# Who adds up the weights: a fused attention and two-layer feed-forward kernel without accumulating transfers in its input projections

## The chip, the cores and the metric

The kernel runs on one core of a Trainium2 chip. TensorE (PE) multiplies matrices into PSUM banks; VectorE (DVE), ScalarE (ACT) and GpSimd (POOL) work element by element; transfers are issued from SyncE's queue (SP) or from GpSimd's (POOL). The metric is the device time of one execution in microseconds, the median of several runs. Before the change it is 526.03 us (three runs, 525.88 to 526.29).

## The reference

Causal attention over 2 batches, 12 heads, 448 positions and 64 dimensions, and then two feed-forward layers on 896 tokens of 768 features, with 2048 features inside:

```python
attn = softmax(mask(q @ k.T / 8)) @ v
x = attn.transpose(0, 2, 1, 3).reshape(896, 768)
h = x @ w1_in;  x = (h * clip(h + 3, 0, 6) / 6) @ w1_out
h = x @ w2_in;  y = (max(h, 0) + alpha * min(h, 0)) @ w2_out
```

All inputs and the output are float32. The weights reach the kernel as 64-bit words, from which it makes 32-bit ones itself.

## The kernel before

**The arithmetic.** Every float32 operand is split into a high part (fp32r) and a low part, the rest; a product of two operands is three matrix multiplications: high by high, high by low, low by high (`three`, L575 to L590). On top of that each of the four large products is done by a scheme of Strassen's kind: 2 × 2 blocks are multiplied with seven products in place of eight, which needs sums and differences of blocks beforehand. The blocks of the activations are made in `take_x`, those of the weights in `w_in` (L592 to L690) and `w_out` (L692 to L787).

**The input projections.** A layer's `w_in` runs for 8 pairs of weight blocks, `w1` and `w2`, each of 128 × 768. `convert` (L249) loads each one with a transfer from SP's queue into a `raw` buffer, of which there are three, and makes 32-bit words of it with two ScalarE instructions (L262, L265) and one on VectorE (L268). Then there are four sums of 384 columns in a pair. The first two are always on VectorE: `s12[right] = w2[left] + w2[right]` (L599) and `s12[left] = s12[right] + w1[left]` (L601). The other two, `w1[right] += s12[left]` and `w2[left] += w1[left]` (L626 and L627), go through the helper `add_on` (L301): either GpSimd issues a transfer inside SBUF that adds on arrival (L307), or VectorE adds (L309). In the trace the first of the two as a transfer is `wf<-s`, the second `wf<-wf`. What comes out is split into high and low parts: ScalarE rounds (L617), VectorE subtracts (L618). Seven products per pair fill three PSUM banks, `a`, `b` and `c`, by turns; ScalarE's copies (L319, L321) and VectorE's additions (L650) empty them, and L660 to L670 apply the activation. The results are the tiles `g`.

**The output projections.** `w_out` makes sums of 768 columns of the weights (`onto`, L702) and of 448 columns of `g` (`add_g`, L728) through the same `add_on`, and differences on VectorE (L707); it splits them (L283, L290) and adds up seven products over 16 tiles. L770 adds finished banks to `y`.

**The order.** Nothing is written in the order in which it runs. Each step is an `Op` with a list of engines and an estimate for each; `Plan.solve` (L113) simulates the engines with these estimates and fixes the order and the engine of each instruction. A step's due time is worked out backwards from the steps that need it, less the estimate of the first engine in its list, and for a transfer less its landing estimate (L119 to L122). For `add_on` the landing estimate is `WAIT[cols]` plus 0.0025 us per column; for a load it is the two numbers in `.lands(2.3, 1.9)`. Where a step may go either way, it is a transfer if that would be done 3.0 us (`EARLY`) before its due time, and otherwise goes to the engine that would be done first:

```python
if POOL in o.dma and done_by(*o.on[0]) + o.on[-1][1] <= o.due - EARLY:
    ok = e == POOL
else:
    ok = e == min(o.on, key=lambda c: done_by(*c))[0]
```

`SEEDS` is a list of random seeds: the first one draws two settings of the planner and shifts the due times of all the attention's steps, each of the others shifts those of some of them. The engines then run their instructions strictly in the order that the plan gave each, and semaphores make them wait for one another.

The functions as they were before the change, with the line numbers of the profile:

Of the kernel before, what the change touches and what calls it, by code (L numbers as in the profile page):

```python
# [24 lines left out]
W3 = HK * P  # L25
# [7 lines left out]
PE, DVE, ACT, POOL, SP = "PE", "DVE", "ACT", "POOL", "SP"  # L33


def f32(t):
    return t.bitcast(F32)
# [23 lines left out]

ISSUE, WAIT = 0.9, {384: 2.2, 448: 4.6, 768: 4.2}

TURN = {("r", "r"): 0.05, ("r", "t"): 0.17, ("r", "c"): 0.2, ("r", "q"): 0.15, ("r", "m"): 0.15, ("t", "r"): 0.12,
        ("t", "c"): 0.12, ("t", "q"): 0.1, ("m", "c"): 0.2, ("m", "r"): 0.1, ("m", "q"): 0.1}
# [14 lines left out]
class Plan:  # L82
# [4 lines left out]
    def op(self, on, emit, reads=(), writes=(), due=FAR, chain=None, also=(), port=False, mode=None):  # L87

        o = Op(on if isinstance(on, list) else [on], emit, due)
        o.port, o.mode = port, mode  # L90
        for key in reads:
            w, r = self.state.setdefault(key, ([], []))
            o.before.update(w)
            r.append(o)
        for key in writes:
            w, r = self.state.setdefault(key, ([], []))
            o.before.update(w)
            o.before.update(r)
            self.state[key] = ([o], [])
        o.before.discard(o)  # L100
        for key in (*reads, *writes, *also):
            b = key[0] if isinstance(key, tuple) else key
            if b not in o.bufs:
                o.bufs.append(b)
                b.left += 1
        if chain:
            if chain in self.last:
                o.before.add(self.last[chain])
            self.last[chain] = o
        self.ops.append(o)  # L110
        return o
# [127 lines left out]
class Kernel:  # L239
# [9 lines left out]
    def convert(self, src, sign=1.0, halves=False):  # L249

        nc, op = self.nc, self.plan.op
        raw = Buf("raw", "raw", 2 * DM, U32)
        w = Buf("w", "wf", DM, U32)
        keys = [(w, 0), (w, W3)] if halves else [w]

        def words(k):
            return raw.tile.rearrange("p (n two) -> p n two", two=2)[:, :, k]

        op((SP, 0.45), lambda e: nc.sync.dma_start(out=raw.tile, in_=src), writes=[(raw, "l"), (raw, "h")]).lands(2.3, 1.9)


        op((ACT, 0.80), lambda e: nc.scalar.activation(  # L262
            f32(w.tile), f32(words(1)), AF.Prelu, scale=sign * 2.0 ** -112, alpha=-2.0 ** 32), reads=[(raw, "h")], writes=keys)

        op((ACT, LOWEST), lambda e: nc.scalar.activation(  # L265
            words(0), raw.tile.bitcast(U16).rearrange("p (n four) -> p n four", four=4)[:, :, 1],
            AF.Copy, bias=-0.49999, scale=1.0 / 8192.0), writes=[(raw, "l")])
        op((DVE, 0.87), lambda e: nc.vector.scalar_tensor_tensor(  # L268
            out=w.tile, in0=w.tile, scalar=3, in1=words(0), op0=ALU.logical_shift_left, op1=ALU.bitwise_or),
           reads=[(raw, "l")], writes=keys, port=True)  # L270
        return w
# [26 lines left out]
        op(low_on, low, reads=[*keys, hi], writes=[lo], port=not ps)  # L298
        return hi, lo

    def add_on(self, out, cols, dst, src, reads, writes, send=False):  # L301

        nc = self.nc

        def emit(e):
            if e == POOL:
                nc.gpsimd.dma_start(out=dst(), in_=src(), accum_op=ALU.add)  # L307
            else:
                nc.vector.tensor_add(dst(), dst(), src())  # L309

        on = [(POOL, ISSUE), (DVE, 0.065 + 0.00105 * cols)]
        self.plan.op(on[:1] if send else on, emit, reads=reads, writes=writes, port=True).lands(WAIT[cols], 0.0025 * cols, on=POOL)

    def copy(self, out, src, key, cols, sign=1.0):
        nc = self.nc
# [276 lines left out]
    def w_in(self, layer, m, src, due):  # L592
        nc, op = self.nc, self.plan.op
        w1 = self.convert(src[m], -1.0, True)
        w2 = self.convert(src[m + PAIRS], 1.0, True)
        s12 = Buf("w", "s12", DM, F32)
        left, right = slice(0, W3), slice(W3, DM)

        op((DVE, 0.47), lambda _: nc.vector.tensor_add(s12.tile[:, right], f32(w2.tile[:, left]), f32(w2.tile[:, right])),  # L599
           reads=[(w2, 0), (w2, W3)], writes=[(s12, W3)], port=True)  # L600
        op((DVE, 0.47), lambda _: nc.vector.tensor_add(s12.tile[:, left], s12.tile[:, right], f32(w1.tile[:, left])),  # L601
           reads=[(s12, W3), (w1, 0)], writes=[(s12, 0)], port=True)

        def both(name, cols, src, keys):

            if cols == DM:
                hi, lo = Buf("w", name + "h", DM, F32R), Buf("w", name + "l", DM, F32R)
                parts = (hi, 0), (lo, 0)
            else:
                t = Buf("w", name, DM, F32R)  # L610
                parts = ((t, 0), 0), ((t, W3), W3)

            def out(i):
                key, first = parts[i]
                return (key[0] if isinstance(key, tuple) else key).tile[:, first:first + cols]

            op((ACT, 0.07 + 0.00087 * cols), lambda _: nc.scalar.copy(out(0), src()), reads=keys, writes=[parts[0][0]])  # L617
            op((DVE, 0.065 + 0.00105 * cols), lambda _: nc.vector.tensor_sub(out(1), src(), f32(out(0))),  # L618
               reads=[*keys, parts[0][0]], writes=[parts[1][0]], port=True)
            return parts  # L620
# [2 lines left out]
        p56 = both("s12", DM, lambda: s12.tile, [(s12, 0), (s12, W3)])  # L623
        p4 = both("a2", W3, lambda: f32(w2.tile[:, right]), [(w2, W3)])

        self.add_on(w1, W3, lambda: f32(w1.tile[:, right]), lambda: s12.tile[:, left], [(s12, 0)], [(w1, W3)], SEND > 1)  # L626
        self.add_on(w2, W3, lambda: f32(w2.tile[:, left]), lambda: f32(w1.tile[:, left]), [(w1, 0)], [(w2, 0)], SEND > 0)  # L627
        p7 = both("s4", W3, lambda: f32(w1.tile[:, right]), [(w1, W3)])
        p3 = both("s3", W3, lambda: f32(w2.tile[:, left]), [(w2, 0)])

# [167 lines left out]
    def build(self):  # L798
        nc, op, d = self.nc, self.plan.op, self.dram
        start, step = 9.0, 5.8  # L800
        warm = Buf("ps", "warm")
        for _ in range(WARM):
            op((PE, 0.9), lambda _: nc.tensor.matmul(
                warm.tile[:, 0:3 * P], lhsT=self.mask[:, 3 * P:4 * P], rhs=self.mask[:, 3 * P:6 * P], start=True, stop=True),
               writes=[warm], due=-90.0)
        for c in range(KIN):
            self.attend(c, [start + (n + 1) * step for n in (2 * c, 2 * c + 1)])
        self.vary = len(self.plan.ops)
        alpha = Buf("alpha", "alpha")
        op((SP, 0.45), lambda _: nc.sync.dma_start(out=self.alpha, in_=d["alpha"]), writes=[alpha], due=start + 20.0).lands(2.1, 0.1)  # L810
        for sign in (1.0, -1.0):
            at = slice(0, KFF) if sign > 0 else slice(KFF, 2 * KFF)
            op((DVE, 0.2), lambda _, sign=sign, at=at: nc.vector.tensor_scalar(
                self.alpha[:, at], self.alpha[:, at], -sign, sign, ALU.mult, ALU.add), writes=[alpha], due=start + 60.0)
        due = start + 2 * KIN * step - 2.0
        for layer, (w_in, w_out) in enumerate((("w1i", "w1o"), ("w2i", "w2o"))):
            for m in range(PAIRS):
                self.w_in(layer, m, d[w_in], due)
            self.w_out(layer, d[w_out], due, self.turned if layer == 0 else self.store)
# [3 lines left out]
OVER = 38  # L823
WARM = 3
SPLIT = (0, 1)
SEND = 0
LOWEST = 0.85
SCALERS = 2
SEEDS = (21, 46993, 49846, 39502, 10980, 46964, 66667)
ATT = {"kq": 2 * S, "v": 8 * D, "e": 3 * P, "el": 4 * P, "small": 21, "a": 16 * P}  # L830


def solve(k):
    return k.plan.solve(SLOTS, ("u", "w", "raw"), ("u", OVER, set(ATT)), k.vary, SEEDS)

# [105 lines left out]
```

## Time and profile before

| | |
|---|---|
| median of three runs | 526.03 us (525.88 to 526.29) |
| the profiled execution, its own time | 521.06 us |
| its span | 519.0 us |
| mean granted clock of TensorE | 0.99 |
| busy: TensorE, VectorE, ScalarE, GpSimd | 96%, 82%, 75%, 25% |
| chain that ended last | TensorE 44%, VectorE 27%, transfers 17%, ScalarE 5% |
| issues of GpSimd's queue at L307 | 48 of `g`, 38 of `wf` |
| transfers | 82.69 MB, 159 GB/s in the mean |

The span runs from the first to the last instruction of the program; the execution's own time has the start and the end around it, some 2 us. A busy share is the part of the span in which an engine had an instruction in it. A matrix multiplication's end is modelled, so the distance from one start to the next tells more than its length. On VectorE too an instruction begins shortly before the one ahead of it has ended. The attention takes the first 85 us or so; the first layer's input projections follow until about 190, its output projections until about 300, the second layer's until about 405 and the end.

### The profile page before, as it was taken

To read this page: it belongs to the slowest core of one execution; us is meant where nothing else is said; L and a number is where in the kernel's file an instruction comes from. 1 tells how busy PE (TensorE), PEld (TensorE's weight loads), DVE (VectorE), ACT (ScalarE), POOL (GpSimd) and SP (SyncE) were. 2 spreads that over 40 slices of the span, in tenths; PEclk is the share of its full clock that TensorE was granted. 3 is DMA by queue.
4 is the path that set the end of the run, shared out by engine and by line. 5 is a ranking of instruction groups with operands and counts; after the bars stand their busy time and mean duration, and the time that the engine had idled before them with its cause. 6 is when DMAs were issued, how large, how long until landed. Compare 5 with 4: busy or idle time off the path is not lost.

```text
span 519.0 us, 7641 instructions
## 1 busy us (share of the span) xinstructions
PE 496.6 (96%) x2598; PEld 429.2 (83%) x2598; DVE 425.1 (82%) x808; ACT 390.5 (75%) x756; POOL 128.7 (25%) x196
## 2 busy tenths in 40 slices
PE   8899999999799999998998897999999999989997
PEld 4575667989689999997997786889999999979996
DVE  5799989999588799878999986887787999699710
ACT  6999999888588799866966676777788997597101
POOL 2775884112111003621001011221210146200000
PEclk9999999999889999999999899999999999999999
DMA  8655300678766549998005436676764699930111
GB/s 273 261 197 167 90 21 24 189 216 218 188 168 167 192 136 276 256 267 251 11 0 153 136 85 162 188 204 148 198 160 153 200 258 273 249 75 1 54 53 53
DMA packets 27638, 82.69 MB, mean 159 GB/s; under 512 B 3152, under 2 KB 15184, under 8 KB 27600
## 3 DMA queue, kind: packets, MB, share of 16 engines
q1 hardware_dynamic: 15216, 61.76, 34.3%
q0 software_dynamic: 12384, 20.45, 22.4%
q8 instruction: 20, 0.33, 0.3%
q14 instruction: 18, 0.15, 0.1%
HBM read 59.00 MB, written 2.75 MB: 119 GB/s over the span
## 4 chain that ended last, share of the span: by engine, by line
PE 44%; DVE 27%; DMA 17%; issue 5%; ACT 5%; POOL 2%; DVEq 0%; POOLq 0%; ACTq 0%; SPq 0%
PE a L584 12%; PE ya L584 12%; DMA g<-g 8%; PE c L584 7%; DMA wf<-s 6%; DVE wf L268 4%; PE b L584 3%; PE yc L584 3%; PE o L565 2%; PE t L521 2%; PE s L496 2%; DVE e L447 2%; DVE g L662 2%; DMA raw<-w2o 1%; DMA raw<-w1o 1%
## 5 line engine op out<-in xcount | busy, mean ns | idle before, releaser
L307 POOL DMA_DIRECT2D g<-g x48 | 41.6, 925 | 146.2 <-DVE g L668 50.3
L268 DVE SCALAR_TENSOR_TENSOR wf<-wf,raw 128x768 uint32<-128x768 uint32 x64 | 60.9, 952 | 15.1 <-ACT wf L262 14.9
L265 ACT ACTIVATE raw<-raw 128x768 uint32<-128x768 uint16 x64 | 58.5, 916 | 4.5 <-DMA raw<-w2i 1.9
L262 ACT ACTIVATE wf<-raw 128x768 f32<-128x768 f32 x64 | 57.5, 903 | 2.8 <-DVE w3l L287 1.4
L307 POOL DMA_DIRECT2D wf<-wf x25 | 21.8, 871 | 133.5 <-DVE s L599 39.4
L452 ACT ACTIVATE e<-e,small 128x128 f32<-128x128 f32 (+2 forms) x72 | 36.0, 505 | 5.1 <-DVE small L447 4.9
L476 POOL TENSOR_SCALAR e<-e,small 128x256 f32<-128x256 f32 (+2 forms) x67 | 31.4, 492 | 15.6 <-DVE small L469 11.0
L447 DVE CUSTOM_DVE_ANT_0 e<-s,mask 128x384 f32<-128x384 f32 (+2 forms) x72 | 27.0, 419 | 6.1 <-PE s L496 5.5
L618 DVE TENSOR_TENSOR s<-wf,s 128x384 fp32r<-128x384 f32 x32 | 17.8, 570 | 10.2 <-ACT s L617 10.2
L319 ACT COPY o<-ya 128x448 f32<-128x448 f32 x3 | 1.6, 533 | 31.6 <-PE ya L584 31.6
L617 ACT CAST s<-wf 128x384 fp32r<-128x384 f32 x32 | 16.1, 507 | 12.0 <-DMA wf<-s 10.2
L565 PE MATMUL o<-a,v 128*64 128x448 f32 (+3 forms) x192 | 23.4, 386 | 0.0
L617 ACT CAST s12h<-s 128x768 fp32r<-128x768 f32 x16 | 13.3, 834 | 13.1 <-DVE s L601 13.1
L565 PEld LDWEIGHTS o<-a,v 128*64 128x64 f32 x192 | 12.7, 136 | 12.6 <-issue 5.2
L496 PE MATMUL s<-kq 64*128 64x384 f32 (+2 forms) x144 | 21.7, 405 | 1.3 <-DMA kq<-kq 0.8
L618 DVE TENSOR_TENSOR s12l<-s,s12h 128x768 fp32r<-128x768 f32 x16 | 15.8, 988 | 7.2 <-ACT s12h L617 6.7
L521 PE MATMUL t<-ident,e 128*128 128x128 f32 x144 | 19.0, 278 | 1.6 <-DVE small L447 1.1
L521 PEld LDWEIGHTS t<-ident,e 128*128 128x128 f32 x144 | 15.5, 141 | 5.5 <-POOL e L476 2.4
L496 PEld LDWEIGHTS s<-kq 64*128 64x128 f32 x144 | 11.6, 186 | 9.2 <-DVE small L447 3.2
L307 POOL DMA_DIRECT2D wf<-s x13 | 11.2, 864 | 25.3 <-DVE s L618 10.7
L668 DVE SCALAR_TENSOR_TENSOR g<-r,alpha,g 128x448 f32<-128x448 f32 x24 | 16.3, 679 | 0.9 <-ACT r L666 0.8
L319 ACT COPY g<-a 128x448 f32<-128x448 f32 x16 | 8.5, 531 | 10.3 <-PE a L584 10.1
(830 smaller groups left out, 1771.3 us busy)
## 6 DMA issues: line engine op xcount, KB each, us to landing
raw<-w1i SPq DMA_DIRECT2D x16, 768.0 KB, 5.4
raw<-w1o SPq DMA_DIRECT2D x16, 768.0 KB, 4.4
raw<-w2i SPq DMA_DIRECT2D x16, 768.0 KB, 4.5
raw<-w2o SPq DMA_DIRECT2D x16, 768.0 KB, 5.0
g<-g POOLq DMA_DIRECT2D x48, 224.0 KB, 9.1
kq<-kq SPq DMA_DIRECT2D x11, 448.0 KB, 5.3
wf<-wf POOLq DMA_DIRECT2D x10, 384.0 KB, 8.8
v<-v SPq DMA_DIRECT2D x12, 256.0 KB, 2.7
```

Source lines behind the costliest of these rows:

```text
L262: op((ACT, 0.80), lambda e: nc.scalar.activation(f32(w.tile), f32(words(1)), AF.Prelu, scale=sign * 2.0 ** -112, alpha=-2.0 ** 32), reads= ...
L265: op((ACT, LOWEST), lambda e: nc.scalar.activation(words(0), raw.tile.bitcast(U16).rearrange("p (n four) -> p n four", four=4)[:, :, 1], A ...
L268: op((DVE, 0.87), lambda e: nc.vector.scalar_tensor_tensor(out=w.tile, in0=w.tile, scalar=3, in1=words(0), op0=ALU.logical_shift_left, op1 ...
L307: nc.gpsimd.dma_start(out=dst(), in_=src(), accum_op=ALU.add)
L447: nc.vector.tensor_tensor_reduce(out=view(), in0=t.tile[:, off:off + cols], in1=self.mask[:, at:at + cols], scale=-SCALE, scalar=3.0e38, o ...
L452: nc.scalar.activation(view(), view(), AF.Exp, bias=small.tile[:, u:u + 1], scale=-1.0, accum_out=small.tile[:, 7 + u:8 + u])
L476: (nc.gpsimd if e == POOL else nc.vector).tensor_scalar(view(), view(), by, 1.0, ALU.mult, ALU.mult)
L496: nc.tensor.matmul(t.tile[:, off:off + (i + 1) * P], lhsT=kq.tile[rows, S + i * P:S + (i + 1) * P], rhs=kq.tile[rows, 0:(i + 1) * P], star ...
L521: nc.tensor.transpose(t.tile[:, at * P:(at + 1) * P], src.tile[:, off:off + P], self.ident)
L565: nc.tensor.matmul(o.tile[side * D:(side + 1) * D, 0:cols], lhsT=v.tile[:, (2 * kc + side) * D:(2 * kc + side + 1) * D], rhs=a.tile[:, at: ...
L584: nc.tensor.matmul(out, lhsT=t.tile[:, first + at:first + at + P], rhs=rhs.tile, start=start and key is hi and rhs is xh, stop=stop and ke ...
L618: op((DVE, 0.065 + 0.00105 * cols), lambda _: nc.vector.tensor_sub(out(1), src(), f32(out(0))), reads=[*keys, parts[0][0]], writes=[parts[ ...
```

## The change

Four things change. `add_on` gets a third setting: `send` below 0 leaves VectorE alone in the list of engines. `w_in` uses it (`SEND = -1`), so all four sums of a pair are VectorE's. The planner's estimates for transfers become longer: `WAIT` from 4.6 to 6.5 us for 448 columns, from 4.2 to 7.0 for 768 (that for 384 has no use any more), and a load's from 2.3 + 1.9 to 3.2 + 2.4; one ScalarE step of `convert` is counted 0.81 in place of 0.85 us. And the seeds are others, four in place of seven, the first one kept.

```diff
-ISSUE, WAIT = 0.9, {384: 2.2, 448: 4.6, 768: 4.2}
+ISSUE, WAIT = 0.9, {384: 6.0, 448: 6.5, 768: 7.0}
...
-        op((SP, 0.45), lambda e: nc.sync.dma_start(out=raw.tile, in_=src), writes=[(raw, "l"), (raw, "h")]).lands(2.3, 1.9)
+        op((SP, 0.45), lambda e: nc.sync.dma_start(out=raw.tile, in_=src), writes=[(raw, "l"), (raw, "h")]).lands(3.2, 2.4)
...
-        op((ACT, LOWEST), lambda e: nc.scalar.activation(
+        op((ACT, 0.81), lambda e: nc.scalar.activation(
...
-    def add_on(self, out, cols, dst, src, reads, writes, send=False):
+    def add_on(self, out, cols, dst, src, reads, writes, send=0):
...
-        self.plan.op(on[:1] if send else on, emit, reads=reads, writes=writes, port=True).lands(WAIT[cols], 0.0025 * cols, on=POOL)
+        self.plan.op(on[:1] if send > 0 else on[1:] if send < 0 else on, emit, reads=reads, writes=writes, port=True).lands(WAIT[cols], 0.0025 * cols, on=POOL)
...
-        self.add_on(w1, W3, lambda: f32(w1.tile[:, right]), lambda: s12.tile[:, left], [(s12, 0)], [(w1, W3)], SEND > 1)
-        self.add_on(w2, W3, lambda: f32(w2.tile[:, left]), lambda: f32(w1.tile[:, left]), [(w1, 0)], [(w2, 0)], SEND > 0)
+        self.add_on(w1, W3, lambda: f32(w1.tile[:, right]), lambda: s12.tile[:, left], [(s12, 0)], [(w1, W3)], SEND)
+        self.add_on(w2, W3, lambda: f32(w2.tile[:, left]), lambda: f32(w1.tile[:, left]), [(w1, 0)], [(w2, 0)], SEND)
...
-SEND = 0
-LOWEST = 0.85
+SEND = -1
-SEEDS = (21, 46993, 49846, 39502, 10980, 46964, 66667)
+SEEDS = (21, 41862, 63962, 88307)
```

## Rows read from the trace of the kernel before

**Rows 1.** The page, part 1: busy time, share of span, instructions of each engine.

```profile
PE 496.6 (96%) x2598; PEld 429.2 (83%) x2598; DVE 425.1 (82%) x808; ACT 390.5 (75%) x756; POOL 128.7 (25%) x196
```

**Rows 2.** Stretches: length, busy us per engine (instructions), granted clock, DMA share, GB/s.

```profile
0.00:85.00 85.00, 80.46 (x596) 50.72 (x597) 69.97 (x260) 76.90 (x235) 55.86 (x112) 1.00 0.46 154
85.00:130.00 45.00, 44.70 (x219) 40.70 (x218) 44.27 (x73) 39.26 (x66) 7.03 (x9) 1.00 0.65 187
130.00:190.00 60.00, 56.26 (x257) 50.41 (x257) 46.02 (x73) 47.79 (x80) 7.74 (x9) 0.94 0.61 170
190.00:240.00 50.00, 49.95 (x242) 45.07 (x241) 42.75 (x65) 38.28 (x63) 18.27 (x21) 1.00 1.01 263
240.00:300.00 60.00, 55.00 (x263) 50.21 (x262) 58.50 (x92) 44.58 (x74) 4.30 (x5) 0.97 0.31 86
300.00:345.00 45.00, 41.56 (x201) 37.10 (x200) 35.18 (x57) 32.10 (x55) 6.93 (x8) 1.00 0.60 164
345.00:400.00 55.00, 55.00 (x273) 50.98 (x272) 43.42 (x68) 42.73 (x72) 9.49 (x11) 1.00 0.62 171
```

**Rows 3.** Waits: who waited for whom, us in total, times, longest.

```profile
ACT s L617 <- DMA wf<-s: 10.2, 4, 3.9
DVE s L618 <- ACT s L617: 10.2, 4, 4.2
...
PE a L584 <- ACT g L321: 5.5, 4, 3.1
PE ya L584 <- DVE y L770: 3.7, 1, 3.7
PE ya L584 <- DVE w6l L290: 2.9, 3, 1.3
PE a L584 <- DVE g L650: 1.8, 1, 1.8
```

**Rows 4.** The chain in order of time: start, us, what; the transfers `wf<-s`.

```profile
125.22 6.30 DMA wf<-s
135.24 6.47 DMA wf<-s
...
312.26 8.21 DMA wf<-s
```

**Rows 5.** Timeline: start, us, instruction, in brackets the idle time before it.

```profile
131.54 0.51 ACT L617 CAST s<-wf 128x384 fp32r<-128x384 f32 x1 [2.52 <-DMA wf<-s]
...
141.74 0.51 ACT L617 CAST s<-wf 128x384 fp32r<-128x384 f32 x1 [3.41 <-DMA wf<-s]
...
143.48 0.48 PE L584 MATMUL a<-t200h,s12h 128*128 128x448 f32 x1 [1.94 <-ACT g L321]
...
320.55 0.51 ACT L617 CAST s<-wf 128x384 fp32r<-128x384 f32 x1 [3.87 <-DMA wf<-s]
```

**Rows 6.** DMA issues of GpSimd's queue: count, KB each, median us to landing.

```profile
g<-g POOLq DMA_DIRECT2D x48, 224.0 KB, 9.1
...
wf<-wf POOLq DMA_DIRECT2D x10, 384.0 KB, 8.8
...
wf<-wf POOLq DMA_DIRECT2D x15, 192.0 KB, 4.3
wf<-s POOLq DMA_DIRECT2D x13, 192.0 KB, 3.8
```

**Rows 7.** Timeline of VectorE: instructions back to back.

```profile
275.74 0.95 DVE L618 TENSOR_TENSOR a1l<-wf,a1h 128x768 fp32r<-128x768 f32 x1
276.61 0.55 DVE L601 TENSOR_TENSOR s<-s,wf 128x384 f32<-128x384 f32 x1
277.08 0.62 DVE L332 TENSOR_TENSOR t<-y,y 128x448 f32<-128x448 f32 x1
```

**Rows 8.** Stretches, POOL's instructions on tile `wf` alone: length, busy (issues).

```profile
85.00:130.00 45.00, 4.35 (x5) 1.00 0.65 187
270.00:300.00 30.00, 3.44 (x4) 0.94 0.44 125
```

## The prediction

> **What bounds the kernel now.** I read the page's engine line first: TensorE is busy 496.6 of 519.0 us, so little can be won at all, and what can be won are the places where it is not fed in time [rows 1]. The stage table shows where they lie: TensorE has next to no air in 85–130, 190–240 and 345–400, and loses 3.7, 5.0 and 3.4 us in 130–190, 240–300 and 300–345 [rows 2]. VectorE's column is to be read beside it: in 85–130 and 240–300 it is full (44.27 of 45, 58.50 of 60), in the other stretches it has 7 to 14 us of air [rows 2]. There are thus two kinds of loss: one where VectorE itself is late, and one where VectorE stands idle too.
>
> The table of waits names the second kind. ScalarE waited 10.2 us in four waits at L617 for the landing of `wf<-s`, an accumulating transfer of an input projection; TensorE's own waits are 5.5 us for a ScalarE copy (L321), 1.8 us for L650, 2.9 us for `w6l` and 3.7 us for L770 [rows 3]. VectorE idled 10.2 us in four waits for the same L617 [rows 3]. These belong together: an engine runs its instructions in order, so while ScalarE stands at L617 for a sum that TensorE does not need yet, the copy that empties TensorE's bank stands behind it. The times show that it is the landing: the transfers issued at 125.22, 135.24 and 312.26 land at 131.52, 141.71 and 320.47 [rows 4], and ScalarE starts at 131.54, 141.74 and 320.55, after 2.52, 3.41 and 3.87 us of idling; TensorE's 1.94 us at 143.48 follows the second of these [rows 5]. The 1.8 us of L650 follows the first, and the longest L321 wait, 3.1 us, the third [rows 3].
>
> There is a second price. The stretch 130–190, with the first two stops in it, has a mean granted clock of 0.94 [rows 2]: the deficit is 0.06 × 60 = 3.6 us, time lost at the lower level of 1.2 GHz. The stretch 300–345, with the longest stop, still reads 1.00 [rows 2], so this price is paid after the first two alone.
>
> **The change part by part.** The code has two sums for each of the 16 pairs that can go either way, 32 in all; the profile has 13 + 15 = 28 of them as transfers of 192 KB, landing after 3.8 and 4.3 us in the median [rows 6]. All 28 go to VectorE.
>
> *What goes.* The three stops that follow a landing: 1.8 + 1.94 + 3.1 = 6.8 us of idling and 3.6 us of slow clock, **−10.4 us**. Also 28 issues on GpSimd; its share is 25% [rows 1] and none of TensorE's waits names it [rows 3], so I take nothing for them. The transfers queue behind the 224 KB ones, which land after 9.1 us [rows 6]; fewer in that queue could help those, but the 48 of `g` bunch in 190–240, where no projection sum is issued, so nothing again.
>
> *What comes.* A 384-column sum on VectorE: L601 starts at 276.61 and the next instruction at 277.08, so 0.47 us [rows 7] (its own duration of 0.55 overlaps the next). 28 × 0.47 = 13.2 us of VectorE work. Where there is air it is free: in 130–190, 300–345 and 345–400 VectorE has 14.0, 9.8 and 11.6 us of it [rows 2] for about 5 or 6 sums, under 3 us, each. That cover would be gone only if the plan crowded work there. Where it is full the work shows: 5 moved sums in 85–130 and 4 in 270–300 [rows 8], 2.35 and 1.9 us. In 240–300 TensorE already waits 3.7 us for a VectorE instruction (L770) that stands behind other VectorE work [rows 3], so the 1.9 us count in full. In 85–130 TensorE is at 44.70 of 45 [rows 2], so VectorE, though full, is a little ahead: between 0 and 2.35 I take 1.2. Together **+3.1 us**.
>
> *The new wait.* ScalarE's rounding (L617) now waits for a VectorE sum instead of a landing, and behind it stand the same bank copies. The sum has to get past what is ahead of it on VectorE, a conversion or two; VectorE idles for nearly the whole of the old waits [rows 3], so the sum would have been done long before. I take 0. Bounds: a gain is excluded, as the stop is already counted whole; the loss is the whole 10.4 us.
>
> *The plan's costs.* The sum's planned lead before its reader falls from 0.9 + 2.2 + 0.96 to 0.47 us, so its producers become 3.6 us less urgent; loads and the other sums are counted 1.4 to 2.8 us longer and become more urgent. The planner had 5.7 us for a sum of `g` (4.6 + 1.12) and 6.1 for a 768-column one; the trace has 9.1 and 8.8 [rows 6], the new costs give 7.6 and 8.9. A plan nearer to the trace should be late less often. Gain at most the `w6l` and L770 waits, 2.9 + 3.7 us [rows 3], and 1.8 us of clock deficit (0.03 × 60) in 240–300 [rows 2]. Loss: longer counted transfers make it choose VectorE more often (10 sums of 768 columns and 48 of `g` still travel [rows 6]); priced below. I take 0, because gain and loss come from the same decision.
>
> *The attention's order* follows the list of seeds; the first is kept, the others differ. TensorE is idle 4.5 us in the first 85 [rows 2], mostly waiting for the first loads; a gain over 1 us is hardly there, a loss of as much is. I take 0.
>
> Sum: −10.4 + 3.1 = −7.3 us. The profiled execution took 521.06 us, its span 519.0; it becomes 513.8. The median of the runs shown is 526.03, 5.0 above the profiled one, so I put the same difference there: **518.7 us**.
>
> The weak term is the length of a transfer. The rows have medians of 3.8 and 4.3 us, and 6.30, 6.47 and 8.21 us in the three stops [rows 4, 6]. The Trainium skill, DMA: Bandwidth & Descriptors, section "Anatomy of one DMA — SWDGE (gpsimd) path", gives 2.0 us plus the bytes over 436 GB/s, an estimate of 2.45 us for 192 KB. By that, each of the three would have landed before ScalarE's wait began, nothing could be won, and the sum would be +3.1 us, 529.1; the rows contradict it for transfers that share the engines with others.
>
> **The rivals.**
> *VectorE becomes the bound (527.7 us, slower).* Place: the output projections, 190–300 and its twin in the second layer. With longer counted landings the planner gives VectorE the sums that travelled: all 5 of 768 columns in a layer (0.87 us each by the distance from 275.74 to 276.61 [rows 7], 4.4 us) and half of the 24 of `g` (0.54 us each by columns, 6.4 us), 10.8 us. 190–240 has 7.3 us of air [rows 2], of which I count 5 as usable; 240–300 has none. So some 5.5 us in the first layer and 3.5 in the second, −7.3 + 9 = +1.7. It decides from about 7 us of moved work in a layer. For it: VectorE at 58.50 of 60. Against: the planner charges VectorE's time quite rightly and spreads it.
> *The output projections recover too (510.3 us).* If the plan with longer landings no longer runs into `w6l` and L770, 2.9 + 3.7 + 1.8 us come on top: −15.7. For it: those waits stand where the landings are twice the planned ones. Against: L770 waits in VectorE's own queue, which gets fuller.
> *The stops stay under another name (525 to 527 us).* The sums are now less urgent by 3.6 us, so they may be placed late, and ScalarE waits for VectorE in place of the landing. For it: L617 still stands ahead of the bank copies. Against: in the old waits VectorE had 10.2 us idle in four pieces, the longest 4.2 [rows 3].
> *The landings were not the cause (529 us).* Then 28 sums come and nothing goes: +3.1. Against it: ScalarE's starts within 0.08 us of the landings [rows 4, 5]. That the change doesn't do what it says I rule out: with a single engine in the list the planner has no choice.
>
> **How the numbers follow.** Forecast 0.55, recovery 0.16, VectorE bound 0.16, stops under another name 0.11, landings not the cause 0.02. The forecast's own range is 515 (no charge for VectorE, 10.4 won, and a little from the attention) to 523.5 (4.25 charged, 6.8 won). The range of 510 to 528.5 takes in the recovery and the VectorE case as worked out and leaves out the worse part of each, about 0.15. A measurement here can tell about 0.2% (1 us) from no change. Faster: 0.54 of the forecast, 0.16 and 0.03 of the third rival, 0.73. The same: 0.07, mostly that rival. Slower: 0.16 + 0.02 + 0.02 = 0.20.
>
> **What would show it.** Right: no `wf<-s` transfer, 32 sums of 384 columns on VectorE at 0.47 us from start to start, no ScalarE wait for a landing in the input projections, TensorE without a stop over 1 us in 130–190 and 300–345 and a clock of 1.00 there, VectorE's busy time up by about 15 us (28 × 0.55). Wrong in the first term: L617 waiting for the sums instead. Wrong in the second: TensorE waits in 85–130 or 240–300 grown by over 3 us. Wrong in the third: fewer than 58 transfers left, VectorE's busy time up by over 20 us, and new `w6l`-like waits.

## The result and the profile after

The changed kernel takes 509.96 us in the median of three runs (508.55 to 510.97) against 526.03: a ratio of 0.969 with a 95% interval of 0.965 to 0.973, 16 us faster where 7.3 were forecast. Two later series with the same kernel on other chips gave 0.963 and 0.964.

| | before | after |
|---|---|---|
| median | 526.03 us | 509.96 us |
| the profiled execution, its own time | 521.06 us | 508.55 us |
| its span | 519.0 us | 506.7 us |
| mean granted clock of TensorE | 0.99 | 1.00 |
| chain that ended last: TensorE, VectorE, transfers | 44%, 27%, 17% | 60%, 23%, 7% |
| transfers | 82.69 MB | 76.79 MB |

The two profiled executions lie 12.5 us apart and the medians 16.1: before's profile was of an execution 5.0 us below its median, after's of one 1.4 us below. A profile explains the 12.5 only; the verdicts below rest on ratios over all executions of a run, each with its interval.

The page's engine line after, which answers to [rows 1]: TensorE's share is up to 97%, VectorE has 27 instructions more and 11.8 us more of work, GpSimd's share is down by a fifth.

```profile
PE 492.1 (97%) x2598; PEld 428.6 (85%) x2598; DVE 436.9 (86%) x835; ACT 391.0 (77%) x760; POOL 101.0 (20%) x165
```

The same stretches as in [rows 2] (length, busy us per engine with its instructions in brackets, granted clock, DMA share, GB/s):

```profile
0.00:85.00 85.00, 80.60 (x584) 51.36 (x584) 67.19 (x257) 76.84 (x238) 47.74 (x104) 1.00 0.44 150
85.00:130.00 45.00, 44.61 (x224) 40.17 (x225) 44.79 (x75) 38.03 (x65) 6.23 (x7) 1.00 0.50 155
130.00:190.00 60.00, 60.00 (x298) 55.66 (x297) 58.34 (x95) 54.28 (x90) 4.32 (x5) 1.00 0.57 180
190.00:240.00 50.00, 50.00 (x249) 46.37 (x248) 45.35 (x65) 39.60 (x66) 17.45 (x20) 1.00 0.98 256
240.00:300.00 60.00, 55.17 (x262) 50.11 (x261) 55.47 (x90) 41.12 (x69) 0.00 (x0) 0.97 0.18 57
300.00:345.00 45.00, 45.00 (x221) 40.82 (x220) 44.52 (x75) 36.80 (x64) 2.60 (x3) 1.00 0.49 156
345.00:400.00 55.00, 54.78 (x270) 50.21 (x269) 47.69 (x76) 46.02 (x78) 4.59 (x6) 1.00 0.53 165
```

In 130–190 TensorE is now busy for all 60.00 us at a granted clock of 1.00 (before 56.26 at 0.94), in 300–345 for all 45.00 (before 41.56). VectorE has almost no air left in three stretches (44.79 of 45, 58.34 of 60, 44.52 of 45), and still TensorE is fed there. Only 240–300 looks as it did: 55.17 at 0.97.

The waits, which answer to [rows 3] (us in total, times, longest):

```profile
PE ya L584 <- DVE y L770: 4.5, 1, 4.5
DVE s L618 <- ACT s L617: 3.2, 4, 2.0
...
ACT s L617 <- DVE wf L309: 1.4, 3, 0.6
...
PE yc L584 <- DVE y L770: 1.4, 1, 1.4
...
PE a L584 <- ACT g L321: 0.3, 1, 0.3
```

ScalarE's 10.2 us at L617 for landings have become 1.4, in three waits of at most 0.6 us, for VectorE's sums at L309; TensorE's 5.5 us for L321 are 0.3, and its waits for L650 and `w6l` are gone. What is left is L770: 4.5 us in 240–300, a little longer than before, and a new wait of 1.4 us at 431, in the second layer. VectorE's sums take what [rows 7] foretold, 0.47 us from start to start:

```profile
100.12 0.55 DVE L309 TENSOR_TENSOR wf<-wf,s 128x384 f32<-128x384 f32 x1
100.59 0.55 DVE L309 TENSOR_TENSOR wf<-wf 128x384 f32<-128x384 f32 x1
101.06 0.94 DVE L268 SCALAR_TENSOR_TENSOR wf<-wf,raw 128x768 uint32<-128x768 uint32 x1
```

**Where the 12.3 us of span went.** I added up the distances between the starts of successive L584 multiplications in each stage, less 203 ns for each, the usual distance: what is left is air and slow clock. In us:

| stage | before | after |
|---|---|---|
| first layer, input projections | 9.1 | 0.8 |
| first layer, output projections | 8.1 | 6.4 |
| second layer, input projections | 4.4 | 1.9 |
| second layer, output projections | 2.6 | 1.5 |
| attention (its time up to its last multiplication, less 203 ns per L584) | 81.9 | 83.1 |

The input projections give 8.3 + 2.5 = 10.8 us, the output projections 2.8, and the attention takes 1.2 back.

### The profile page after: what moved, and what is told of

It reads as the page before. It is cut to its first block, busy times and chain, and to the rows that moved or that the text cites. A ratio compares the mean times of both kernels' runs of the same rounds, so it can differ in the third digit from the quotient of the medians.

```text
span 506.7 us, 7588 instructions
## 1 busy us (share of the span) xinstructions
PE 492.1 (97%) x2598; PEld 428.6 (85%) x2598; DVE 436.9 (86%) x835; ACT 391.0 (77%) x760; POOL 101.0 (20%) x165
## 2 busy tenths in 40 slices
DMA packets 23462, 76.79 MB, mean 152 GB/s; under 512 B 2688, under 2 KB 11136, under 8 KB 23424
## 4 chain that ended last, share of the span: by engine, by line
PE 60%; DVE 23%; DMA 7%; ACT 7%; issue 3%; POOL 1%; DVEq 0%; POOLq 0%; ACTq 0%
PE ya L584 14%; PE a L584 14%; PE c L584 7%; PE yc L584 7%; DMA g<-g 5%; PE o L565 4%; PE b L584 4%; DVE wf L268 3%; PE yb L584 3%; PE s L496 3%; PE t L521 2%; DVE g L668 2%; DVE g L650 2%; ACT e L452 1%; DMA raw<-w2o 1%
## 5 line engine op out<-in xcount | busy, mean ns | idle before, releaser
L476 POOL TENSOR_SCALAR e<-e,small 128x256 f32<-128x256 f32 (+2 forms) x65 | 30.4, 486 | 16.8 <-DVE small L469 10.8
L565 PEld LDWEIGHTS o<-a,v 128*64 128x64 f32 x192 | 13.1, 136 | 14.1 <-ACT a L547 5.3
L496 PE MATMUL s<-kq 64*128 64x384 f32 (+2 forms) x144 | 23.2, 412 | 0.8 <-DVE small L447 0.8
L309 DVE TENSOR_TENSOR wf<-wf 128x384 f32<-128x384 f32 (+1 forms) x31 | 23.3, 750 | 0.3
L666 ACT ACTIVATE r<-g 128x448 f32<-128x448 f32 x24 | 13.9, 577 | 7.9 <-DVE g L650 7.7
L617 ACT CAST s12h<-s 128x768 fp32r<-128x768 f32 x16 | 13.3, 834 | 6.8 <-DVE s L601 6.7
L660 ACT ACTIVATE r<-g 128x448 f32<-128x448 f32 x24 | 13.8, 575 | 6.0 <-DVE g L650 5.9
L617 ACT CAST a1h<-wf 128x768 fp32r<-128x768 f32 x16 | 13.4, 836 | 6.4 <-DVE wf L268 6.4
L617 ACT CAST s<-wf 128x384 fp32r<-128x384 f32 x32 | 16.0, 512 | 1.4 <-DVE wf L309 1.4
L547 ACT COPY a<-t 128x512 f32<-128x512 f32 x30 | 16.4, 594 | 0.3
```

The source lines that it names most:

```text
L476: (nc.gpsimd if e == POOL else nc.vector).tensor_scalar(view(), view(), by, 1.0, ALU.mult, ALU.mult)
L496: nc.tensor.matmul(t.tile[:, off:off + (i + 1) * P], lhsT=kq.tile[rows, S + i * P:S + (i + 1) * P], rhs=kq.tile[rows, 0:(i + 1) * P], star ...
L565: nc.tensor.matmul(o.tile[side * D:(side + 1) * D, 0:cols], lhsT=v.tile[:, (2 * kc + side) * D:(2 * kc + side + 1) * D], rhs=a.tile[:, at: ...
```

## The experiments

Each ratio is to the kernel before on the same chip, with its 95% interval; "the changed kernel" is at 0.963 to 0.969 in this measure. Theory A, as the prediction had it: the sums' landings are what is won. The rivals: the planner's estimates win as much or more; the seeds do; or half of the sums would do.

**1. The sums alone, in the order of before.** The planner's order is kept on every engine; only where GpSimd would have issued a 384-column transfer, VectorE makes the sum.

```diff
-            if e == POOL:
+            if e == POOL and cols != W3:
```

> The order that the plan of before gives is kept on every engine; only the 28 sums of 384 columns that it gave to transfers are VectorE instructions, in the places where GpSimd issued them. Theory A (the landings block ScalarE and VectorE, with TensorE's bank copies queued behind): the stops after 132, 141 and 320 us go and the clock stays at 1.00 in 130 to 190; TensorE's excess over 203 ns from start to start falls by 9 to 11 us in the two input projections; the waits for w6l and for L770 in the output projections stay at about 3 and 4 us; 8 to 11 us faster than before. Theory B (the new costs and seeds, that is the plan, bring the gain): under 3 us faster. Theory C (VectorE is full, 13 us of work more): no change or slower.

Measured: 0.985 (0.979 to 0.991), 519.61 against 527.02 us, so −7.4, a little under the 8 to 11 of theory A. Its waits:

```profile
ACT s12h L617 <- DVE s L601: 18.2, 14, 4.1
...
ACT x46h L283 <- DMA g<-g: 6.3, 2, 3.9
...
PE ya L584 <- DVE y L770: 5.2, 1, 5.2
...
PE ya L584 <- DVE w6l L290: 3.3, 4, 1.3
...
PE ya L584 <- ACT w6h L283: 2.3, 2, 1.8
...
PE a L584 <- DVE g L650: 0.8, 1, 0.8
```

TensorE has no wait for L321 left and ScalarE none for a landing at L617, so the three stops go with the landings, in the same order of work; the granted clock in 130–190 is 1.00. ScalarE still waits at L617 for VectorE's sums of L601 (18.2 us, before 13.1), but the longest stop of TensorE in the input projections is now the 0.8 us for L650. The input projections lose 3.8 and 1.2 us (before 9.1 and 4.4), 8.5 us less where theory A had 9 to 11. What stands in the list now are waits of the output projections, for splits of weights (`w6h`, `w6l`) and for L770; they lose 12.1 and 4.2 us in this one execution (before 8.1 and 2.6). That execution took 520.87 us, 1.3 above its kernel's median, so the stage sums are rather high; that the later stages take part of the gain back is suggested by them, not shown.

**2. The sums alone, in an order of their own.** `send` below 0 as in the change, everything else as before.

```diff
-        self.plan.op(on[:1] if send else on, emit, ...
+        self.plan.op(on[:1] if send > 0 else on[1:] if send < 0 else on, emit, ...
...
-SEND = 0
+SEND = -1
```

> All four sums of a pair are VectorE's, with the planner's costs and the seeds of before. Theory A: 8 to 11 us faster than before, with stops in the output projections as before (waits for w6l and L770 of 3 to 7 us). Theory B: under 3 us. If the sums alone give 14 to 17 us, neither the costs nor the seeds matter.

Measured: 0.985 (0.982 to 0.989), 518.48 against 527.02 us, so −8.5. The planner's knowing of it adds nothing that can be measured to experiment 1.

**3. The estimates alone.** The sums may travel, and 21 of them do.

```diff
-ISSUE, WAIT = 0.9, {384: 2.2, 448: 4.6, 768: 4.2}
+ISSUE, WAIT = 0.9, {384: 2.2, 448: 6.5, 768: 7.0}
...
-.lands(2.3, 1.9)
+.lands(3.2, 2.4)
...
-LOWEST = 0.85
+LOWEST = 0.81
```

> The new planner's costs for the sums of 448 and 768 columns, for loads and for one ScalarE step, with the sums of 384 columns free to travel at the old cost and the old seeds; 21 of them are transfers. Theory A: ScalarE's waits for landings in the input projections stay at 5 us or more; 0 to 5 us faster than before, from the output projections alone (waits for w6l gone). Theory B: 8 us faster or more.

Measured: 0.975 (0.970 to 0.979), theory B's case. More than the sums alone, with 21 transfers still on their way and a ScalarE that still waits for them:

```profile
PE ya L584 <- DVE y L770: 4.7, 1, 4.7
ACT s L617 <- DMA wf<-s: 4.7, 3, 2.2
...
PE a L584 <- ACT g L321: 3.4, 2, 1.9
...
PE ya L584 <- DVE w6l L290: 0.5, 1, 0.5
```

This is what the prediction had at nothing.

**4. The seeds alone**, and **5. the change with the old seeds.**

```diff
-SEEDS = (21, 46993, 49846, 39502, 10980, 46964, 66667)
+SEEDS = (21, 41862, 63962, 88307)
```

> The kernel before with the new seeds and nothing else: 22 or so of the sums are still transfers. Theory A: within 4 us of before, either way, since the landings still block. Theory B in the form that the seeds bring it: 8 us faster or more.

> The changed kernel with the seven seeds of before. As the new seeds alone gave nothing, theory A+ expects it within 0.7% of the changed kernel beside it. If seeds and costs go together, it is over 1% slower.

Measured: 1.001 (0.998 to 1.004), and 0.968 (0.962 to 0.974) without them. The seeds are worth nothing that shows.

**6. All 32 sums as transfers, in the changed kernel's order.**

```diff
-            if e == POOL:
+            if e == POOL or cols == W3:
```

> The changed kernel's own order on every engine, but all 32 sums of 384 columns are transfers issued by GpSimd in the places where VectorE added (13 us of VectorE's work less). Theory A (a sum on VectorE is what the gain needs, as ScalarE stands still until a transfer lands): ScalarE's waits for landings at L617 rise to 30 us or more, and the time is 10 us or more above the changed kernel's, so 520 us or worse. Theory B (the plan's costs bring the gain, whoever adds): within 3 us of the run with the costs alone, 510 to 517 us. Theory C (VectorE's load is what still limits): faster than the changed kernel.

Measured: 1.081 (1.074 to 1.088). The mechanism in reverse, in an order that was planned without transfers: waits for landings, and behind them the same chain, five to six times as long as before.

```profile
DVE s L618 <- ACT s L617: 43.4, 23, 6.0
ACT s L617 <- DMA wf<-s: 41.2, 15, 6.0
...
PE a L584 <- ACT g L321: 20.0, 7, 9.4
...
PE a L584 <- ACT g L319: 15.3, 6, 6.2
...
ACT s L617 <- DMA wf<-wf: 12.7, 9, 5.6
```

ScalarE stands for 53.9 us at L617 for landings, and TensorE for 35.3 behind bank copies.

**7. The changed kernel, but the sums may travel** if the planner, with its new estimate of 6.0 us, likes it (15 do).

```diff
-SEND = -1
+SEND = 0
```

> The changed kernel with the sums of 384 columns free to travel again, counted at the longer landing (6.0 us and 0.96): 15 are transfers. If a transfer does no harm once it is counted at its true length: within 3 us of the changed kernel, 507 to 513 us, with ScalarE's waits for landings in the input projections under 2 us. If it does harm in any plan: 514 us or more.

Measured: 0.983 (0.977 to 0.990), slower than the changed kernel by some 1.5 to 2%. ScalarE waits only 0.7 us for a landing at L617 here; TensorE's waits in the input projections are of about 1 us each, and ScalarE has waits of 5.3 us for loads. In its profiled execution, whose span is 7.4 us longer than the changed kernel's, the first layer's input projections lose 7.3 us by the sum of distances (the changed kernel's 0.8), with a granted clock of 0.96 in 85–130. So hardly any of it is a wait for a sum; why the time goes there is open.

**8. The two estimates apart:** the load's alone, and those of the longer sums alone.

```diff
-.lands(2.3, 1.9)
+.lands(3.2, 2.4)
```

> The kernel before with one estimate changed, the loads' from 2.3 and 1.9 to 3.2 and 2.4 us. The run with the costs alone gained 13 us; if the loads' estimate is its larger part, this one is 7 us or more faster than before and the stops in the input projections are smaller; if the sums' estimate is, it is within 4 us of before.

```diff
-ISSUE, WAIT = 0.9, {384: 2.2, 448: 4.6, 768: 4.2}
+ISSUE, WAIT = 0.9, {384: 2.2, 448: 6.5, 768: 7.0}
```

> The kernel before with the estimates of the sums of 448 and 768 columns alone changed, 4.6 to 6.5 and 4.2 to 7.0 us. If they carry the gain of the costs: 7 us or more faster than before, waits for w6l and w6h in the output projections under 1 us; ScalarE's waits for landings at L617 stay as before, at 8 us or more, as nothing about them is changed. If the loads' estimate carries it: within 4 us of before.

Measured: 0.977 (0.968 to 0.986) for the load's, 0.998 (0.994 to 1.003) for the sums'. The load's estimate alone does as much as experiment 3, within an interval of ±0.9%, and the sums' does nothing.

**9. The two parts that count, together:** the sums on VectorE and the load's estimate, all else as before. Beside it the changed kernel again.

```diff
-SEND = 0
+SEND = -1
...
-.lands(2.3, 1.9)
+.lands(3.2, 2.4)
```

> Two parts of the change: the four sums of a pair on VectorE and the loads' estimate of 3.2 and 2.4 us; the sums' estimates, the ScalarE estimate and the seeds are those of before. Theory A+ (these two carry the gain, each for its own stops): 0.965 to 0.978 of before. If the estimates of the sums of 448 and 768 columns are needed beside them: 0.98 or more, with waits for w6l or w6h of over 3 us.

> The changed kernel once more, for the ratio on the same chip as the runs beside it: 0.965 to 0.975 of before.

Measured: 0.969 (0.964 to 0.974), beside 0.963 (0.959 to 0.968). These two parts make the change, all but a difference of half a per cent that the intervals do not settle. By the same sums of distances as above, the output projections lose 5.8 and 2.4 us in its profiled execution, where experiment 2's has 11.4 and 3.6 and before's 8.1 and 2.6. By these single executions it is there that the load's estimate wins, and hardly in the input projections (3.1 and 1.2 us, experiment 2: 1.4 and 3.6).

**10. Is it the loads, or only a luckier order?** First by dose: experiment 9 with the load's estimate, 5.6 us in total, at 4.9 and at 7.0.

```diff
-.lands(3.2, 2.4)
+.lands(2.75, 2.15)
```

> The run with the sums and the loads' estimate, with that estimate half way, 2.75 and 2.15 us, 4.9 in all. If the gain comes from counting the loads more nearly at their true length, this lies between the runs at 4.2 and 5.6 us (0.985 and 0.969 of before): 0.972 to 0.982. If every new estimate only shuffles the order, it can be anywhere between 0.965 and 0.995.

```diff
-.lands(3.2, 2.4)
+.lands(4.0, 3.0)
```

> The same with the loads counted 4.0 and 3.0 us, 7.0 in all, longer than the page's medians of 4.4 to 5.4 us. If the estimate has to be near the true length: 0.972 or more of before. If longer is only safer: 0.965 to 0.971, with ScalarE's waits for loads under 1.5 us.

Measured: 0.981 (0.976 to 0.987) and 0.968 (0.961 to 0.975). With 4.2 us at 0.985 and 5.6 at 0.969, the series falls and then is flat: by these four points the estimate has to be long enough, not near the true length. The page of the kernel before has the loads' landings (count, KB, median us to landing); all four medians are above the planned 4.2 us, to which the planner adds only what it foresees of queueing, and below 5.6:

```profile
raw<-w1i SPq DMA_DIRECT2D x16, 768.0 KB, 5.4
raw<-w1o SPq DMA_DIRECT2D x16, 768.0 KB, 4.4
raw<-w2i SPq DMA_DIRECT2D x16, 768.0 KB, 4.5
raw<-w2o SPq DMA_DIRECT2D x16, 768.0 KB, 5.0
```

Then without touching the plan: the order of experiment 2, planned for 4.2 us, but the transfers bring half the bytes, and ScalarE's two steps read that half twice.

```diff
-dma_start(out=raw.tile, in_=src)
+dma_start(out=raw.tile[:, 0:DM], in_=src[:, 0:DM])
...
-            f32(w.tile), f32(words(1)), AF.Prelu, ...
+            split2(f32(w.tile)), twice(f32(words(1)[:, 0:W3])), AF.Prelu, ...
```

> The order of the run with the sums alone on every engine, but each of the 64 weight loads moves 384 KB in place of 768; ScalarE's two steps of a conversion read the loaded half twice, so the weights are not the reference's and the work of the engines is the same size. Theory L (the loads themselves land too late for the order that the old estimate gives): ScalarE's waits for loads and for the sums of g shrink, the stops at w6l and w6h go, and the ratio to before falls from 0.985 to 0.965 to 0.975, as with the longer estimate. Theory O (the estimate acts through the order alone, and the loads are on time as they are): 0.98 to 0.988, with the stops in the output projections still there.

Measured: 0.965 (0.958 to 0.972), where the same order with whole loads had 0.985. The transfers and waits of experiment 2, with TensorE's longest stop and the wait of ScalarE ahead of it (start, us, instruction, idle time before it):

```profile
raw<-w1o SPq DMA_DIRECT2D x16, 768.0 KB, 6.2
...
raw<-w2o SPq DMA_DIRECT2D x16, 768.0 KB, 5.2
g<-g POOLq DMA_DIRECT2D x48, 224.0 KB, 9.6
```

```profile
PE ya L584 <- ACT w6h L283: 5.4, 2, 4.4
...
ACT x45h L283 <- DMA g<-g: 4.9, 2, 4.1
...
PE ya L584 <- DVE w6l L290: 3.3, 3, 1.6
...
ACT raw L265 <- DMA raw<-w2o: 3.2, 4, 1.4
```

```profile
231.18 0.57 ACT L283 CAST x45h<-g 128x448 fp32r<-128x448 f32 x1 [4.11 <-DMA g<-g]
...
238.28 0.74 PE L584 MATMUL ya<-x62h,w6h 128*128 128x448 f32 x1 [4.38 <-ACT w6h L283]
```

and with half loads (line numbers are higher by six):

```profile
g<-g POOLq DMA_DIRECT2D x48, 224.0 KB, 5.8
...
raw<-w1o SPq DMA_DIRECT2D x16, 384.0 KB, 3.2
...
raw<-w2o SPq DMA_DIRECT2D x16, 384.0 KB, 3.2
```

```profile
PE ya L590 <- DVE y L776: 2.3, 1, 2.3
...
PE ya L590 <- DVE w6l L296: 1.0, 1, 1.0
```

The waits for `w6h` are gone and those for `w6l` are a third. So an order planned for 4.2 us is a good one if the loads land in 3.2; with the true loads it is not. The sums of `g` land sooner too, 5.8 us in place of 9.6, so this run does not tell the loads' own lateness from what they do to the transfers beside them.

The trace of experiment 2 speaks for the second in one place: the 4.38 us stop at 238 comes after ScalarE has stood for landings of sums of `g`, with the conversion of a load and `w6h` behind them in its order; its waits for loads are of at most 1.4 us. Experiment 9 has no stop at `w6h` any more, though its sums of `g` still land after 8.6 us in the median:

```profile
ACT x66h L283 <- DMA g<-g: 5.7, 2, 3.4
...
PE ya L584 <- DVE w6l L290: 2.7, 3, 1.4
...
ACT raw L265 <- DMA raw<-w2o: 0.8, 2, 0.4
```

That the load's estimate and the bytes of the loads are each worth their per cents is shown. Whether the estimate wins because loads are no longer late, or because the new order puts less behind the waits for sums of `g`, is not. Nor is every new order a measure of its estimate: experiments 7 and 12 have orders that are 1.3 to 2% slower than the changed kernel's for no cause found. Against mere luck stand the two bases (experiments 8 and 9), the series of four and the half loads in an unchanged order.

**11. What is left: L770 in 240–300.** In the changed kernel the stop looks like this (start, us, instruction, idle time before it):

```profile
277.45 0.62 DVE L290 TENSOR_TENSOR t312l<-t,t312h 128x448 fp32r<-128x448 f32 x1
277.99 1.15 DVE L770 TENSOR_TENSOR y<-y,ya 128x448 f32<-128x448 f32 x2
278.65 0.64 PE L584 MATMUL ya<-x30h,w3h 128*128 128x448 f32 x1 [4.50 <-DVE y L770]
```

L770 stands behind other VectorE work. In the first layer it is moved some six VectorE instructions forward, with its product's steps.

```diff
+                if o.on[0] == (DVE, 0.54) and any(b in y22 for b in o.bufs) and any(b in a for b in o.bufs):
+                    o.sooner = SOONER - 0.1
...
-        return sorted(done, key=lambda o: (o.start, o.index))
+        return sorted(done, key=lambda o: (o.start - o.sooner, o.index))
```

> The changed kernel, but in the first layer the three VectorE additions at L770 that free the banks for the last product stand six instructions earlier in VectorE's order, as if the plan had expected the product before them 3.5 us sooner; TensorE's order is the same. If the 4.5 us stop after 273 us is nothing but these additions standing behind work that is not needed yet, it goes with the clock deficit behind it: 4 to 6 us faster than the changed kernel beside it, and no new stop over 1 us at the start of the second layer. If VectorE as a whole is late there, what is passed over is late instead: within 1.5 us of the changed kernel, with a stop at 290 to 300 us in its place.

Measured: 0.964 (0.960 to 0.968) beside 0.963 (0.959 to 0.968) for the changed kernel. The wait fell from 4.1 us to 1.0, another of 1.4 came, and the time stayed. In the profiled execution the clock deficit went with the wait (1.00 in 240–300, 0.97 in the changed kernel beside it), but that execution, 510.38 us, was the longest of its six and ran much of its way at the slower pace told in the last section. The intervals exclude the 4 to 6 us that were hoped for, not one or two.

**12. Longer estimates in the changed kernel:** the sums' (8.5 and 9.5 us), and the load's (7.0), beside the changed kernel a third time.

```diff
-ISSUE, WAIT = 0.9, {384: 6.0, 448: 6.5, 768: 7.0}
+ISSUE, WAIT = 0.9, {384: 6.0, 448: 8.5, 768: 9.5}
```

> The changed kernel with the sums that still travel counted 2.0 and 2.5 us longer again, 8.5 and 9.5 us before their columns, nearer to the 9 to 14 us that they take in the output projections. If the stops that are left there (L770 after 273 and 429 us) come from landings later than the plan's: 3 us or more faster than the changed kernel, under 0.960 of before. If VectorE is what is full there: 0.962 to 0.970, with nine sums of 768 columns or fewer travelling.

```diff
-.lands(3.2, 2.4)
+.lands(4.0, 3.0)
```

> The changed kernel with the loads counted 4.0 and 3.0 us, 7.0 in all. If a longer estimate for loads only makes the order safer, it is 1 to 3 us faster than the changed kernel beside it; if 5.6 us is already past the point from which it pays, it is within 2 us of it; if the conversions are then placed so early that VectorE misses its bank copies, it is slower, with longer waits for L770.

> The changed kernel again, as the measure on the same chip: 0.962 to 0.971 of before.

Measured: 0.977 (0.972 to 0.982), 0.968 (0.962 to 0.973), and 0.964 (0.959 to 0.968). Sums of `g` land after 8.9 us in the changed kernel's median, and still an estimate nearer to that is worse than either case expected; why is open. No version measured is clearly faster than the changed kernel.

## Why the prediction was wrong

**The first term, −10.4 us, held.** The three stops and the slow clock of 130–190 are gone, and by the stage table the input projections give 10.8. Experiment 1 shows that the landings were the cause (8.5 us in the input projections), experiment 6 shows it from the other side. *The new wait*, taken at 0, held too: ScalarE waits 1.4 us at L617 for the sums. One reading behind the first term was wrong and did no harm: only 17 of the 48 transfers of `g` are issued in 190–240, 17 more in the second layer's output projections, and 14 in the input projections, beside the sums of 384 columns. They land after 8.9 us where it was 9.1, so nothing came of that.

**VectorE's charge, +3.1, was too high for the changed kernel.** In 85–130 nothing came of the 1.2 us: VectorE is full to 44.79 of 45, and TensorE is at 44.61 after 44.70. In 240–300 L770 waits 4.5 us after 3.7, 0.8 us where 1.9 stood; the other new wait, 1.4 us, lies at 431 in the second layer, where nothing was charged. A full VectorE was no bound here: in 130–190 it is busy 58.34 of 60 us and TensorE 60.00. With the old estimate for loads there was a price: in the one profiled execution of each, the output projections of experiments 1 and 2 lose 5.6 and 4.3 us more than before's. Whether VectorE's extra work is its cause is not shown. VectorE's busy time rose by 11.8 us, less than the 15 foretold.

**The sum of both, −7.3, is what the sums alone bring:** −7.4 us in experiment 1, −8.5 in experiment 2.

**The step that failed is "The plan's costs", with its "I take 0, because gain and loss come from the same decision".** They do not. The loss I priced, more work for VectorE, did not come: 57 of 58 transfers stayed. The gain was in a number that this step named only in passing: the load's estimate. I compared the planner's figures for sums with their landings and never those for loads, 4.2 us against medians of 4.4 to 5.4. The runs give 2.3% for it alone and 1.6% on top of the sums, some 8.5 us, with nothing for the sums' estimates or the seeds (both taken at 0, rightly). The step's own upper bound, 8.4 us, is about what came, but not from the waits that it counted, as L770 stayed. The estimate wins in the output projections, and by which path from the loads to TensorE is open (experiment 10).

**The offset.** The forecast put before's distance of median to profile, 5.0 us, on the changed kernel. It is 1.4. Of the 8.7 us between 518.7 and 509.96, 3.6 are this and 5.2 are the terms (513.8 foretold for a profiled execution, 508.55 measured). Before's later medians, 524 to 528, say that its profiled execution was a short one, so part of its losses was probably not in the trace that I read. (TensorE's 4.5 us in the attention, which were put down mostly to the first loads, are only 0.8 us of waiting for a load; the term of 0 does not hang on it.)

**The rivals.** "The output projections recover too" came within half a microsecond (510.3), by half its mechanism: the `w6l` waits are gone, as it said, but L770 and the clock of 0.97 stayed. That the time fits is partly luck: L770's 3.7 and the clock's 1.8 us, which it counted, did not come, and the 3.6 of the offset, which it did not count, did. Experiment 11 adds that L770's wait was not worth its length in time. "VectorE becomes the bound" had the full VectorE right, and not its price. "The stops under another name" are 1.4 us of ScalarE's waits in all.

**The weak term.** The estimate worked out from the Trainium skill, DMA: Bandwidth & Descriptors, section "Anatomy of one DMA — SWDGE (gpsimd) path", for 192 KB was 2.45 us, and 529.1 us would have followed. No run shows it here: with 15 sums travelling (experiment 7) the medians are 3.1 and 5.2 us, and the ScalarE waits for landings in experiment 6 are of up to 6.0.

## What to carry to other kernels

Where a planner orders the work, put each of its estimates beside the measured landing before anything else, the loads first: here one that lay 0.2 to 1.2 us under the medians cost about as much as the three stops that could be seen, and no single wait pointed to it. But measure each change of an estimate by itself: one that came nearer to its landings gained nothing, and then cost 1.3%. An engine that runs in order should wait for a transfer only if nothing that another engine needs stands behind it. A long wait in the list need not be worth its length: try it by taking it alone.

## What was not expected of the hardware

The distance from one L584 multiplication to the next is 203 ns in most stretches and 207 ns in others, 10 to 200 us long, with a granted clock of 1.00 in both. The chain of the kernel before has both (start, us, nine multiplications): 1.86 us early, 1.82 late.

```profile
148.98 1.86 PE a L584 x9
...
341.40 1.82 PE a L584 x9
```

In before the slower pace lasts from 148 to 237 us, with shorter pieces elsewhere, and costs 1.6 us in that stretch; in experiment 11's profile, from 100 to 298 and 346 to 430, it costs 4.7; in the changed kernel's profile it is some 30 us long in all, most of it from 280 to 300, and costs about 0.5. In experiment 9's profile of the changed kernel the longest piece lies elsewhere, from about 330 to 352, so its place goes with the execution and not with the kernel. It may be part of why one kernel's runs lie several microseconds apart. What causes it no run shows.

The clock did not fall after every stop: 300–345 in before, with the stop of 3.1 us that ends at 324, has a granted clock of 1.00, and 130–190, with two stops of under 2 us, has 0.94 [rows 2, 3, 5].
